# Merging attention and feed-forward sums of three query chunks, and sending score tiles in pairs by another rule, in a fused transformer block

## The chip, the cores and the metric

The kernel runs on one core of one Trainium2 chip. The metric is the device time of one execution in microseconds (us). A core has TensorE (PE, with its weight loads PEld), VectorE (DVE), ScalarE (ACT), GpSimd (POOL) and SyncE (SP, which issues the DMAs here). The records also give for each run the mean clock that was granted to TensorE, as a share of full speed.

## The reference, cut to what matters

```python
# x: 1 x 2048 x 512 (bf16); 32 heads of 16; feed-forward width 1792
xn = layernorm(x)
q, k, v = split(xn @ wqkv)
p = softmax(einsum("bhqd,bhkd->bhqk", q, k) * 16 ** -0.5)
attn = einsum("bhqk,bhkd->bhqd", p, v) @ wo
h = silu(xn @ w1) * (xn @ w3)
return x + attn + h @ w2
```

Of the kernel before, what the change touches and what calls it, by code (L numbers as in the profile page):

```python
# [9 lines left out]
ALU = mybir.AluOpType  # L10
# [1027 lines left out]
def _plan_fast(nc, ps, flag, A_x, A_wqkv, A_wo, B_w1, B_w3, B_w2, out):  # L1038
# [15 lines left out]
    NR = NU * RPU  # L1054
    NV = NU + 1
    NPR = 12
    NON = 6
    NP = NG // 2
    G_LO = 352.0
# [14 lines left out]
    A_SOON = 0.7  # L1074
    D_SOON = 0.6
    D_RIDE = 1.0
    A_OVER = 0.1
    A_EARLY = 0.1
    WARM = 36
    VB0 = 24  # L1080
# [10 lines left out]
    with ctx:  # L1091
# [8 lines left out]
        lnt = sb("lnt", [128, NT], FP32)  # L1100
        mhalf = sb("mhalf", [128, NT], FP32)
        xnT = sb("xnT", [128, DC, S], BF16)
        hT = sb("hT", [128, FC, 512], BF16)
        wq = sb("wq", [128, DC, D], BF16)
        wkv = sb("wkv", [128, 2, DC, D], BF16)
        wk = wkv[:, 0]
# [428 lines left out]
        def tiles_FFN(sc, fc):  # L1535
            idx = sc * FC + fc
            sl = idx % NW
            ss = idx % 2

            def mk(which):  # L1540
                gr = []
                for c in range(DC):
                    gr.append((lambda e, bk, c=c: col_groups(
                        lambda i: w13[:, sl, which * DC + c, 32 * i:32 * i + 32],
                        xnT[:, c, sc * 512:(sc + 1) * 512], 512)(e, bk, c == 0, c == DC - 1),
                        [("w13", sl, which)] + xk(sc * 512, 512), None, DG))
                return gr

            def start():
                if idx + NW - 1 < NQC * FC:  # L1550
                    P.post("sp", lambda: load_w13(idx + NW - 1), ready=P.t, prio=3)

            def evac_g(bk, o, rel):
                def e1():
                    q = P.op("act", lambda e: e.activation(th[:, ss, :], bank(bk), ACTF.Tanh, scale=0.5),  # L1555
                             reads=[("ps", bk)], writes=[("th", ss)], dur=a_cost(512))

                    def e2():
                        q2 = P.op("dve", lambda e: e.scalar_tensor_tensor(t1[:, ss, :], th[:, ss, :], 1.0, bank(bk),  # L1559
                                                                          ALU.add, ALU.mult),  # L1560
                                  reads=[("th", ss), ("ps", bk)], writes=[("t1", ss)], dur=d_cost(512))
                        done[("t1", idx)] = q2.end
                        rel(q2)
                    P.post("dve", e2, ready=q.end + _LAT, prio=1)
                P.post("act", e1, ready=o.end + _LAT, prio=0)

            def evac_u(bk, o, rel):
                def e1():
                    q = P.op("dve", lambda e: e.scalar_tensor_tensor(hT[:, fc, :], t1[:, ss, :], 0.5, bank(bk),  # L1569
                                                                     ALU.mult, ALU.mult),  # L1570
                             reads=[("t1", ss), ("ps", bk)], writes=[("hT", fc)], dur=d_cost(512))
                    done[("hT", sc, fc)] = q.end + _LAT
                    rel(q)
                P.post("dve", e1, ready=o.end + _LAT, prio=1, cond=lambda: ("t1", idx) in done)

            def cond_g():
                if not have(("w13", idx)):
                    return False
                if not xdone(sc * 512, 512)():
                    return False  # L1580
                if sc > 0 and not all(("HF", (sc - 1) * 4 + i) in done for i in range(4)):
                    return False
                return True
            return [_T("G%d_%d" % (sc, fc), mk(0), evac_g, cond=cond_g, start=start),
                    _T("Y%d_%d" % (sc, fc), mk(1), evac_u, cond=lambda: ("G%d_%d" % (sc, fc)) in done)]

# [9 lines left out]
        def tile_OUT(tg, part):  # L1596
            qc, ts = divmod(tg, 4)

            def og(g, slot, key):
                return (lambda i: onorm[:, slot, ts * 128 + 32 * i:ts * 128 + 32 * i + 32], wo[:, g, :],  # L1600
                        [("ON", slot, ts // 2), ("wor", g)],
                        lambda: have(key))
            ffn = [(lambda i, fc=fc: hT[:, fc, ts * 128 + 32 * i:ts * 128 + 32 * i + 32], w2[:, fc, :],
                    [("hT", fc), ("w2", fc)], None) for fc in range(FC)]
            ats = [og(g, (qc * NP + g) % NON, ("ON", qc, g)) for g in range(NP)]
            last_b = [og(NP - 1, ON_B, ("ON", qc, "B", ts // 2))]
            res = [(lambda i: ident[:, 32 * i:32 * i + 32], xr[:, ts % 2, :], [("ident",), ("xr", ts % 2)],
                    lambda: have(("xl", tg)))]
            na = NP - 2 if ts < 1 else NP - 1
            gr = {2: ats[na:] + last_b, 3: ffn + ats[:na] if qc == NQC - 1 else ffn, 4: ats,  # L1610
                  5: ffn + res + ats + last_b}[part]
            groups = []
            for k, (lh, rh, rd, cd) in enumerate(gr):
# [2 lines left out]
            def evac(bk, o, rel):  # L1616
                def e1(eng="dve"):
                    if part == 3:
# [4 lines left out]
                        done[("XE", tg)] = q.end  # L1623
                        rel(q)
                        return
                    if part == 5:
                        q = P.op("act", lambda e: e.activation(osb[:, ts, :], bank(bk), ACTF.Identity),
                                 reads=[("ps", bk)], writes=[("osb", ts), ("xn", ts)], dur=a_cost(512))
                    else:
                        q = P.op("dve", lambda e: e.tensor_tensor(osb[:, ts, :], bank(bk), osum[:, ts, :], ALU.add),  # L1630
                                 reads=[("ps", bk), ("osum", ts)], writes=[("osb", ts), ("xn", ts)], dur=d_cost(512))
                    rel(q)
                    done[("XE", tg)] = q.end
                    if part == 4:
                        P.post("sp", lambda: P.dma(lambda e: e.dma_start(out_v[:, tg, :], osb[:, ts, :]),
                                                   reads=[("osb", ts)], writes=[("out", tg)], kb=128),
                               ready=q.end + _LAT, prio=1)
                        return
# [7 lines left out]
                if part == 5:  # L1646
                    P.post("act", lambda: e1("act"), ready=o.end + _LAT, prio=1)
                else:
                    P.post("dve", e1, ready=o.end + _LAT, prio=1, cond=lambda: part in (2, 4) or ("xr", tg) in done)

            def cond():
                if part == 4:
                    return have(("OSUM", tg), ("ON", qc, NP - 1))
                if part == 2:
                    return have(("OSUM", tg)) and late()
                if not have(*[("hT", qc, fc) for fc in range(FC)]):
                    return False
                if part == 3 and qc > 0 and ("OUT", (qc - 1) * 4 + ts) not in done:
                    return False
                if part == 3:  # L1660
                    return have(*[("KTm", NP - 1, i_) for i_ in range(NQC)])
                return part == 5 or have(("ON", qc, NP - 1))

            def start():
# [2 lines left out]
                    done[("xr", tg)] = P.t  # L1667
                    done[("xl", tg)] = P.dma_last[(P.ndma - 1) % _NDMA_SEMS].end + 0.5
                P.post("sp", load, ready=P.t, prio=1, cond=lambda: tg < 2 or ("XE", tg - 2) in done)
            return _T("O%d_%d" % (tg, part), groups, evac, cond=cond, start=None if part in (2, 4) else start)  # L1670


        st = {"dbl": 0, "pos": 0, "pv": 0, "dbal": 0, "nd": 0, "lastA": -1.0, "n_exp": 0, "wait_a": 0, "hold_d": 0, "last_par": 0, "p1_at": -1.0, "p1_op": None}
# [41 lines left out]
        for sc in range(NQC):  # L1715
            for fc in range(FC):
                bg.extend(tiles_FFN(sc, fc))
            if sc > 0:
                for ts in range(4):
                    bg.append(tile_OUT(sc * 4 - 4 + ts, 4))  # L1720
            for ts in range(4):
                bg.append(tile_OUT(sc * 4 + ts, 5 if sc == NQC - 1 and ts > 2 else 3))
        for ts in range(3):
            bg.append(tile_OUT((NQC - 1) * 4 + ts, 2))
        bank_free = {b: 0.0 for b in range(7)}
# [98 lines left out]
        def try_a():  # L1824
# [7 lines left out]
                    return False  # L1832
                st["dbl"] = 2
            two = len(free) > 1
            if not two and not st["early"]:
                due = max(P.t, P.free["act"]) + 0.905 * st["wait_a"] - A_SOON
                if due > P.t and sorted(pbuf)[1] <= due + A_OVER:
                    return False
# [3 lines left out]
            if two and not st["early"]:  # L1842
                one_a(free[1], st["last_par"])
            return True

        def one_a(buf, avoid):
            nx = a_next(avoid)
# [38 lines left out]
            return None  # L1886

        def d_due():
            if P.free["dve"] - P.t > (D_RIDE if P.pem[0] == "row" and P.t < P.pem[2] + 0.1 else D_SOON):
                return False  # L1890
            sl = dcur[0]
            if sl is None:
# [314 lines left out]
        def start_tile(urgent_only):  # L2207
# [10 lines left out]
                tl = src[2]  # L2218
            elif not urgent_only:
                tl = None  # L2220
                cand = bg[:4 if st["pos"] >= NR else 3] + [x for x in bg[3:] if x.name[0] == "O" and x.name.endswith("_4")]
                if cand and any(z[0] == 0 for z in crit[:4]):
                    cand = []
                cand.sort(key=lambda x: not x.name.endswith("_4"))
                for x in cand:
                    if x.cond is None or x.cond():
                        tl = x
                        break
                if tl is None:
                    return  # L2230
                bg.remove(tl)
            else:
                return
# [7 lines left out]
        def try_dense():  # L2241
            start_tile(False)
            for a in active:
# [6 lines left out]
                if not a.groups:  # L2250
# [5 lines left out]
                    if a.name[0] == "O":  # L2256
                        tg_, pt_ = a.name[1:].split("_")
                        if pt_ != "3":
                            done[("OUT", int(tg_))] = o.end
                        if pt_ in "35":  # L2260
                            done[("HF", int(tg_))] = o.end
                    a.evac(bk, o, rel)
                return True
            return False
# [144 lines left out]
```

## The kernel before: the parts that the change touches

The program is static. A planner written in Python runs through a model of the five engines, decides at each moment what every engine issues next, and so fixes the order on every engine; the times of its model only choose that order. 2048 queries are cut into four chunks of 512. Scores are made in tiles of 128x1024 (two heads' groups side by side, two PSUM banks). Such a tile goes either to ACT, one exponential, or to DVE, which builds an approximate exponential from integer steps: a first step `p1` out of PSUM for each tile, then four steps m, t, g, e on two tiles together. There are three PSUM buffers for score tiles (six banks), one bank for dense work and one for the product with V.

How a score tile for ACT or DVE is sent (cut):

```python
def try_a():
    ...
    two = len(free) > 1                       # free: score buffers that are empty
    if not two and not st["early"]:
        due = max(P.t, P.free["act"]) + 0.905 * st["wait_a"] - A_SOON
        if due > P.t and sorted(pbuf)[1] <= due + A_OVER:      # A_SOON 0.7, A_OVER 0.1
            return False                      # another buffer comes free soon: wait, send two
    ...
def d_due():
    if P.free["dve"] - P.t > (D_RIDE if P.pem[0] == "row" and P.t < P.pem[2] + 0.1 else D_SOON):
        return False                          # D_SOON 0.6, D_RIDE 1.0
    ...
```

Two score tiles that are sent one after the other form one run of row-tiled matmuls on TensorE (row-tiled, 32*128 in the lists of groups: each matmul has 32 input rows and is placed at one of the rows 0, 32, 64, 96 of TensorE's array; column-tiled, 128*32 or 128*17 there, as nearly everything else here: 32 output rows or fewer, placed at one of the columns 0, 32, 64, 96).

The output tiles (cut). For every 128 rows of a chunk, the feed-forward product was summed in one PSUM group (part 3, 14 groups of four column matmuls) and moved with the residual to `osum` by DVE; later the attention product was summed in another (part 4, four groups) and a second DVE instruction added `osum`:

```python
hT = sb("hT", [128, FC, 512], BF16)           # FC = 14 hidden-state slots: one chunk
...
gr = {2: ats[na:] + last_b, 3: ffn + ats[:na] if qc == NQC - 1 else ffn, 4: ats,
      5: ffn + res + ats + last_b}[part]
...
if part == 3:
    q = P.op("dve", lambda e: e.tensor_tensor(osum[:, ts, :], bank(bk), xr[:, ts % 2, :], ALU.add), ...)
...
else:
    q = P.op("dve", lambda e: e.tensor_tensor(osb[:, ts, :], bank(bk), osum[:, ts, :], ALU.add), ...)
```

The hidden state of the next chunk could be written as soon as part 3 of this chunk had read the slots; attention did not have to be through.

## Time and profile before

| | kernel before |
|---|---|
| median of the first three runs (range) | 790.03 us (788.83 to 790.27) |
| busy: PE, DVE, ACT | 95%, 97%, 98% of 788.1 us |
| exponentials on ACT; score tiles on DVE | 796; 228 |
| DVE sums of 128x512 for the output | 30 |
| score runs on PE (instruction order) | 745 |

A line of the groups reads: source line, engine, operation, output<-input, shapes, count; then busy time in us and the mean of one in ns; then the engine's idle time just before them and what ended most of it. The prediction below shows the lines.

### The profile page before, as it was taken

The page shows a single profiled execution, that of the slowest core. Times are in us where ns is not written, and L with a number is a line of the kernel's source. Part 1 is how long each engine was busy: PE and PEld are TensorE (multiplying, and loading weights), DVE is VectorE, ACT ScalarE, POOL GpSimd, SP SyncE. Part 2 cuts the span into 40 slices and gives each one's busy share as a digit, 9 for nine tenths or more (in the row PEclk, how much of TensorE's full clock was granted, in tenths as well). Part 3 has the DMA queues.
Part 4 walks back from the last instruction along what each step waited for, and adds up shares of the span by engine and source line. Part 5 has one row for each costly group of instructions (what it writes and reads, how often), then busy time and mean ns, then how long its engine had stood idle before and what let it go on. Part 6 is the DMA issues. An engine that isn't in the chain of part 4 may idle for free.

```text
span 788.1 us, 21640 instructions
## 1 busy us (share of the span) xinstructions
PE 747.1 (95%) x9337; PEld 226.8 (29%) x9337; DVE 764.8 (97%) x1023; ACT 768.5 (98%) x870; POOL 90.7 (12%) x120
## 2 busy tenths in 40 slices
PE   8999999999999999999999999999899999999997
PEld 6422222222222222222222222222222222222234
DVE  8899999999999999999999999999999999999995
ACT  6999999999999999999999999999999999999994
POOL 3200021002020010201102020010201103010000
PEclk9999999999999999999999999999999999999999
DMA  7023122322332222333302234322222332232121
GB/s 215 2 22 115 9 36 30 49 21 40 51 43 22 30 41 38 47 49 45 50 14 34 22 55 56 41 35 38 34 29 23 56 43 39 49 52 16 20 25 33
DMA packets 83441, 32.94 MB, mean 42 GB/s; under 512 B 72072, under 2 KB 79496, under 8 KB 83336
## 3 DMA queue, kind: packets, MB, share of 16 engines
q1 hardware_dynamic: 83336, 31.46, 28.0%
q8 instruction: 75, 1.23, 0.6%
q14 instruction: 30, 0.25, 0.1%
HBM read 22.81 MB, written 2.10 MB: 32 GB/s over the span
## 4 chain that ended last, share of the span: by engine, by line
ACT 82%; PE 11%; DVE 5%; issue 0%; DMA 0%; POOL 0%; DVEq 0%; ACTq 0%
ACT f_PT L1866 78%; PE ps L1332 4%; PE ps L1803 4%; ACT f_th L1555 3%; PE ps L2066 3%; DVE f_xd L1939 1%; DVE f_xd L1988 1%; DVE f_xd L2003 0%; DVE f_xd L1981 0%; DMA f_xd<-in_A_x_dram 0%; DVE f_hT L1569 0%; PE ps L1344 0%; DVE f_t L1559 0%; DVE f_stats L1256 0%; DVE f_xd L1997 0%
## 5 line engine op out<-in xcount | busy, mean ns | idle before, releaser
L1866 ACT ACTIVATE f_PT<-ps 128x1024 bf16<-128x1024 f32 x796 | 744.7, 1151 | 3.4 <-PE ps L1803 3.2
L1803 PE MATMUL ps<-f_QT,f_KT 32*128 32x512 bf16 (+1 forms) x2112 | 313.6, 378 | 23.3 <-ACT f_PT L1866 17.2
L1939 DVE TENSOR_SCALAR f_xd<-ps 128x1024 int16<-128x1024 f32 x228 | 277.2, 1216 | 2.8 <-PE ps L1803 2.5
L2066 PE MATMUL ps<-f_PT,f_Vaug 128*17 128x512 bf16 (+2 forms) x1640 | 205.1, 378 | 1.1 <-DVE f_U L2086 0.5
L2066 PE MATMUL ps<-f_xd,f_Vaug 128*32 128x512 bf16 (+2 forms) x1416 | 181.9, 377 | 4.6 <-DVE f_U L2086 3.1
L1803 PEld LDWEIGHTS ps<-f_QT,f_KT 32*128 32x128 bf16 x2112 | 80.5, 91 | 322.0 <-ACT f_PT L1866 262.1
L1332 PE MATMUL ps<-f_xnT,f_w 128*32 128x512 bf16 x1792 | 143.1, 386 | 3.7 <-DVE f_t L1559 1.6
L1988 DVE TENSOR_TENSOR f_xd<-f_xd 128x2048 bf16<-128x2048 bf16 (+1 forms) x115 | 139.7, 1215 | 0.0
L1471 POOL TENSOR_SCALAR f_QT<-f_QT,f_msk 128x256 bf16<-128x256 bf16 x60 | 55.3, 922 | 270.5 <-DVE f_xd L1997 112.8
L1981 DVE TENSOR_SCALAR f_xd<-f_xd 128x2048 int16<-128x2048 int16 (+1 forms) x115 | 78.1, 679 | 3.9 <-PE ps L2066 3.1
L2003 DVE TENSOR_SCALAR f_xd<-f_xd 128x2048 int16<-128x2048 int16 (+1 forms) x115 | 78.3, 681 | 0.0
L1997 DVE TENSOR_SCALAR f_xd<-f_xd 128x2048 int16<-128x2048 int16 (+1 forms) x115 | 78.2, 680 | 0.0
L1332 PE MATMUL ps<-f_w,f_hT 128*32 128x512 bf16 x896 | 73.2, 383 | 0.2 <-DVE f_xn_sb L1630 0.2
L2127 POOL TENSOR_TENSOR f_onorm<-f_U,f_R 128x256 bf16<-128x256 f32 x30 | 25.4, 854 | 375.6 <-DMA f_R<-f_Rrow 255.0
L2066 PEld LDWEIGHTS ps<-f_PT,f_Vaug 128*32 128x32 bf16 (+1 forms) x1640 | 51.3, 92 | 58.6 <-issue 45.1
L2066 PEld LDWEIGHTS ps<-f_xd,f_Vaug 128*32 128x32 bf16 (+1 forms) x1416 | 46.1, 92 | 49.0 <-issue 28.5
L1332 PEld LDWEIGHTS ps<-f_xnT,f_w 128*32 128x32 bf16 x1792 | 36.6, 95 | 65.2 <-issue 56.5
L1555 ACT ACTIVATE f_th<-ps 128x512 f32<-128x512 f32 x56 | 40.4, 722 | 0.0
L1569 DVE SCALAR_TENSOR_TENSOR f_hT<-f_t,ps 128x512 bf16<-128x512 bf16 x56 | 37.9, 678 | 1.2 <-PE ps L1332 0.8
L1559 DVE SCALAR_TENSOR_TENSOR f_t<-f_th,ps 128x512 bf16<-128x512 f32 x56 | 37.9, 676 | 0.2
L1332 PEld LDWEIGHTS ps<-f_w,f_hT 128*32 128x32 bf16 x896 | 19.1, 95 | 23.1 <-issue 16.4
L1332 PE MATMUL ps<-f_wo,f_onorm 128*32 128x512 bf16 x272 | 22.1, 383 | 0.3 <-DVE f_wkv L1619 0.2
(82 smaller groups left out, 246.1 us busy)
## 6 DMA issues: line engine op xcount, KB each, us to landing
f_w<-in_B_w_dram SPq DMA_DIRECT2D x112, 128.0 KB
f_R<-f_Rrow SPq DMA_DIRECT2D x124, 32.0 KB
f_xr<-in_A_x_dram SPq DMA_DIRECT2D x16, 128.0 KB
f_U<-f_U SPq DMA_DIRECT2D x60, 32.0 KB
f_w<-in_B_w_dram SPq DMA_DIRECT2D x7, 256.0 KB
f_xd<-in_A_x_dram SPq DMA_DIRECT2D x3, 512.0 KB
out_dram<-f_xn_sb SPq DMA_DIRECT2D x12, 128.0 KB
f_xd<-in_A_x_dram SPq DMA_DIRECT2D x2, 256.0 KB
```

The lines of the kernel that those rows point to most:

```text
L1332: ins = e.matmul(bank(bk)[32 * i:32 * i + 32, 0:ncols], make_lhsT(i), rhs_ap, start=start, stop=stop, tile_position=(0, 32 * i))
L1471: q = P.op("pool", lambda e: e.tensor_scalar(QT[:, d_, cs], QT[:, s1, cs], msk[:, h:h + 1], None, ALU.mult), reads=[("QT", s1), ("msk", h) ...
L1555: q = P.op("act", lambda e: e.activation(th[:, ss, :], bank(bk), ACTF.Tanh, scale=0.5), reads=[("ps", bk)], writes=[("th", ss)], dur=a_cos ...
L1559: q2 = P.op("dve", lambda e: e.scalar_tensor_tensor(t1[:, ss, :], th[:, ss, :], 1.0, bank(bk), ALU.add, ALU.mult), reads=[("th", ss), ("ps ...
L1803: ins = e.matmul(b, l_, r_, start=True, stop=True, tile_position=(rp, 0))
L1866: q = P.op("act", lambda e: e.activation(PT[:, s_, :], ps[:, b0 * 512:(b0 + 2) * 512], ACTF.Exp, scale=ASC, bias=ABIAS), reads=[("ps", b0) ...
L1939: q = P.op("dve", lambda e: e.tensor_scalar(dsl[:, ys, 1024 * c:1024 * c + 1024], ps[:, b0 * 512:b0 * 512 + 1024], YB, G_LO, ALU.add, ALU. ...
L1981: P.op("dve", lambda e: e.tensor_scalar(dsl[:, NY + m_, 0:n], y, 0x7F, 0x3F00, ALU.bitwise_and, ALU.bitwise_or), reads=YK, writes=[("ds", ...
L1988: q_ = P.op("dve", lambda e: e.tensor_tensor(t_ap.bitcast(BF16), y.bitcast(BF16), t_ap.bitcast(BF16), ALU.mult), reads=YK + [("ds", NY + m ...
L1997: q_ = P.op("dve", lambda e: e.tensor_scalar(g_ap, y, -G_LO, 0.0, ALU.add, ALU.max), reads=YK, writes=[("g", g_, k) for k in range(n // 51 ...
L2003: q_ = P.op("dve", lambda e: e.tensor_scalar(y, y, 0x7F80, None, ALU.bitwise_and), reads=YK, writes=YK, dur=s_cost(n), name="e", lock=True)
L2066: ins = e.matmul(bank(PV)[32 * j:32 * j + (17 if g % 2 == 0 else 32), pc], v_, p_, start=s0, stop=s1, tile_position=(0, 32 * j))
```

## The change

It has two parts. First, for the first three chunks the feed-forward and the attention product go into one PSUM group (part 0) that DVE moves once, together with the residual. Since the group must wait for attention of its chunk, the ring of hidden-state slots grows from 14 to 20, so the feed-forward part can run six slots ahead. Second, another rule decides when a single score tile is held back for a partner: ACT's tile longer (0.4 us over its due time instead of 0.1), DVE's tile also; with two buffers free, DVE's tile may go 1.4 us ahead of its due time instead of 0.6; and a tile that can join a row run just started is not held. The aim is less DVE work, and fewer switches between row and column tiles on TensorE (in the chain before, eight column matmuls that followed scores took 0.55 us, at 0.22 us per four otherwise).

```diff
+    NH = 20
...
-    A_OVER = 0.1
+    D_TWO = 1.4
+    D_OVER = 0.3
+    A_OVER = 0.4
...
-        hT = sb("hT", [128, FC, 512], BF16)
+        hT = sb("hT", [128, NH, 512], BF16)
...
-                if sc > 0 and not all(("HF", (sc - 1) * 4 + i) in done for i in range(4)):
+                if idx >= NH and not all(("OUT", (idx - NH) // FC * 4 + i) in done for i in range(4)):
                     return False
...
-            gr = {2: ats[na:] + last_b, 3: ffn + ats[:na] if qc == NQC - 1 else ffn, 4: ats,
+            gr = {0: ffn + ats, 2: ats[na:] + last_b, 3: ffn + ats[:na] if qc == NQC - 1 else ffn,
                   5: ffn + res + ats + last_b}[part]
...
+                    if part == 0:
+                        q = P.op("dve", lambda e: e.tensor_tensor(osb[:, ts, :], bank(bk), xr[:, ts % 2, :], ALU.add),
...
-            if not two and not st["early"]:
+            if not two and not st["early"] and not riding():
                 due = max(P.t, P.free["act"]) + 0.905 * st["wait_a"] - A_SOON
...
         def d_due():
-            if P.free["dve"] - P.t > (D_RIDE if P.pem[0] == "row" and P.t < P.pem[2] + 0.1 else D_SOON):
+            n = len(open_bufs())
+            if P.free["dve"] - P.t > (D_RIDE if riding() else D_TWO if n > 1 else D_SOON):
+                return False
+            if n == 1 and not riding() and sorted(pbuf)[1] <= P.free["dve"] + D_OVER:
                 return False
...
-                cand = bg[:4 if st["pos"] >= NR else 3] + [x for x in bg[3:] if x.name[0] == "O" and x.name.endswith("_4")]
+                rest = [x for x in bg if not x.name.endswith("_0")]
+                cand = [x for x in bg if x.name.endswith("_0")] + rest[:4 if st["pos"] >= NR else 3]
```

(`riding()` says that a row run was started within the last 0.1 us.)

More of the change, by code (lines that the diff above doesn't have):

```diff
@@ L1568, in e1 @@
                 def e1():
-                    q = P.op("dve", lambda e: e.scalar_tensor_tensor(hT[:, fc, :], t1[:, ss, :], 0.5, bank(bk),
+                    q = P.op("dve", lambda e: e.scalar_tensor_tensor(hT[:, idx % NH, :], t1[:, ss, :], 0.5, bank(bk),
                                                                      ALU.mult, ALU.mult),
-                             reads=[("t1", ss), ("ps", bk)], writes=[("hT", fc)], dur=d_cost(512))
+                             reads=[("t1", ss), ("ps", bk)], writes=[("hT", idx % NH)], dur=d_cost(512))
                     done[("hT", sc, fc)] = q.end + _LAT
@@ L1602, in og @@
                         lambda: have(key))
-            ffn = [(lambda i, fc=fc: hT[:, fc, ts * 128 + 32 * i:ts * 128 + 32 * i + 32], w2[:, fc, :],
-                    [("hT", fc), ("w2", fc)], None) for fc in range(FC)]
+            ffn = [(lambda i, fc=fc: hT[:, (qc * FC + fc) % NH, ts * 128 + 32 * i:ts * 128 + 32 * i + 32], w2[:, fc, :],
+                    [("hT", (qc * FC + fc) % NH), ("w2", fc)], None) for fc in range(FC)]
             ats = [og(g, (qc * NP + g) % NON, ("ON", qc, g)) for g in range(NP)]
@@ L1625, in e1 @@
                         return
-                    if part == 5:
+                    if part == 0:
+                        q = P.op("dve", lambda e: e.tensor_tensor(osb[:, ts, :], bank(bk), xr[:, ts % 2, :], ALU.add),
+                                 reads=[("ps", bk), ("xr", ts % 2)], writes=[("osb", ts), ("xn", ts)], dur=d_cost(512))
+                    elif part == 5:
                         q = P.op("act", lambda e: e.activation(osb[:, ts, :], bank(bk), ACTF.Identity),
@@ L1633, in e1 @@
                     done[("XE", tg)] = q.end
-                    if part == 4:
+                    if part == 0:
                         P.post("sp", lambda: P.dma(lambda e: e.dma_start(out_v[:, tg, :], osb[:, ts, :]),
@@ L1648, in evac @@
                 else:
-                    P.post("dve", e1, ready=o.end + _LAT, prio=1, cond=lambda: part in (2, 4) or ("xr", tg) in done)
+                    P.post("dve", e1, ready=o.end + _LAT, prio=1, cond=lambda: part == 2 or ("xr", tg) in done)
             def cond():
-                if part == 4:
-                    return have(("OSUM", tg), ("ON", qc, NP - 1))
                 if part == 2:
@@ L1656, in cond @@
                 if not have(*[("hT", qc, fc) for fc in range(FC)]):
-                    return False
-                if part == 3 and qc > 0 and ("OUT", (qc - 1) * 4 + ts) not in done:
                     return False
@@ L1669, in start @@
                 P.post("sp", load, ready=P.t, prio=1, cond=lambda: tg < 2 or ("XE", tg - 2) in done)
-            return _T("O%d_%d" % (tg, part), groups, evac, cond=cond, start=None if part in (2, 4) else start)
+            return _T("O%d_%d" % (tg, part), groups, evac, cond=cond, start=None if part == 2 else start)
         st = {"dbl": 0, "pos": 0, "pv": 0, "dbal": 0, "nd": 0, "lastA": -1.0, "n_exp": 0, "wait_a": 0, "hold_d": 0, "last_par": 0, "p1_at": -1.0, "p1_op": None}
@@ L1717, in _plan_fast @@
                 bg.extend(tiles_FFN(sc, fc))
-            if sc > 0:
-                for ts in range(4):
-                    bg.append(tile_OUT(sc * 4 - 4 + ts, 4))
             for ts in range(4):
-                bg.append(tile_OUT(sc * 4 + ts, 5 if sc == NQC - 1 and ts > 2 else 3))
+                bg.append(tile_OUT(sc * 4 + ts, 0 if sc < NQC - 1 else 5 if ts > 2 else 3))
         for ts in range(3):
@@ L1844, in try_a, with riding @@
             return True
+        def riding():
+            return P.pem[0] == "row" and P.t < P.pem[2] + 0.1
         def one_a(buf, avoid):
@@ L2220, in start_tile @@
                 tl = None
-                cand = bg[:4 if st["pos"] >= NR else 3] + [x for x in bg[3:] if x.name[0] == "O" and x.name.endswith("_4")]
+                rest = [x for x in bg if not x.name.endswith("_0")]
+                cand = [x for x in bg if x.name.endswith("_0")] + rest[:4 if st["pos"] >= NR else 3]
                 if cand and any(z[0] == 0 for z in crit[:4]):
                     cand = []
-                cand.sort(key=lambda x: not x.name.endswith("_4"))
                 for x in cand:
@@ L2259, in try_dense @@
                             done[("OUT", int(tg_))] = o.end
-                        if pt_ in "35":
-                            done[("HF", int(tg_))] = o.end
                     a.evac(bk, o, rel)
```

## The prediction

> **What bounds the kernel now.** I read the busy times first. Three engines are nearly full at once, so the page alone does not name the bound.
>
> ```profile
> span 788.1 us, 21640 instructions
> ...
> PE 747.1 (95%) x9337; PEld 226.8 (29%) x9337; DVE 764.8 (97%) x1023; ACT 768.5 (98%) x870; POOL 90.7 (12%) x120
> ```
>
> ScalarE (ACT) lacks 788.1 - 768.5 = 19.6 us. Cut into 40 us windows, ACT is busy 40.00 of 40.00 us in all but four of twenty. Of the idle time, 8.1 us lie in the first 30 us, 1.3 us between 280 and 320 us, and the rest at the end. The groups and the waits of ACT say the same:
>
> ```profile
> L1866 ACT ACTIVATE f_PT<-ps 128x1024 bf16<-128x1024 f32 x796 | 744.7, 1151 | 3.4 <-PE ps L1803 3.2
> L1939 DVE TENSOR_SCALAR f_xd<-ps 128x1024 int16<-128x1024 f32 x228 | 277.2, 1216 | 2.8 <-PE ps L1803 2.5
> L1803 PE MATMUL ps<-f_QT,f_KT 32*128 32x512 bf16 (+1 forms) x2112 | 313.6, 378 | 23.3 <-ACT f_PT L1866 17.2
> ```
>
> ```profile
> ACT f_PT L1866 <- PE ps L1803: 3.2, 5, 1.3
> ```
>
> A score tile (128x1024) goes to ACT for an exponential (796 of 1024) or to VectorE (DVE) for an integer approximation (228). Ahead of all 796 exponentials ACT waited for scores only five times, 3.2 us in all. The score matmuls, by contrast, wait for ACT to empty a PSUM buffer. So ACT paces the steady part. The third view is the chain of work that ended last:
>
> ```profile
> 30.43 82.58 ACT f_PT L1866 x90
> 113.50 6.42 ACT f_PT L1866 x7
> 120.41 9.17 ACT f_PT L1866 x10
> ...
> 739.06 0.22 PE ps L1332 x4
> 739.28 0.33 PE ps L1803 x4
> 739.61 0.76 PE ps L2066 x12
> 740.36 0.32 PE ps L1803 x2
> 740.68 0.55 PE ps L1332 x8
> ```
>
> 82.58 / 90 gives the true price of an exponential: 0.917 us, not the mean of 1151 ns, since neighbours overlap. Between two runs 120.41 - (113.50 + 6.42) = 0.49 us pass: that is one tanh of the feed-forward part. The chain stays on ACT to about 730 us, then on TensorE (PE) to 780 us; both are full there. Last, a stretch of the timeline of DVE gives its prices, from start to start:
>
> ```profile
> 755.05 0.68 DVE L1619 TENSOR_TENSOR f_wkv<-ps,f_xr 128x512 f32<-128x512 f32 x1
> 755.64 1.21 DVE L1939 TENSOR_SCALAR f_xd<-ps 128x1024 int16<-128x1024 f32 x1
> 756.78 0.68 DVE L2086 COPY f_U<-ps 128x512 f32<-128x512 f32 x1
> 757.37 0.68 DVE L1981 TENSOR_SCALAR f_xd<-f_xd 128x2048 int16<-128x2048 int16 x1
> 757.97 0.68 DVE L1997 TENSOR_SCALAR f_xd<-f_xd 128x2048 int16<-128x2048 int16 x1
> 758.58 1.21 DVE L1939 TENSOR_SCALAR f_xd<-ps 128x1024 int16<-128x1024 f32 x1
> ```
>
> A 128x512 sum out of PSUM costs 0.60 us, the first step on a score tile 1.14, and a step on two tiles (128x2048) 0.60; the product in the chain (L1988) costs 1.13 by the same reading. Two tiles on DVE so cost 2 x 1.14 + 1.13 + 3 x 0.60 = 5.21 us; a chain of one tile 1.14 + 0.60 + 3 x 0.34 = 2.76 us.
>
> [...] Scores use row tiles, everything else here column tiles. [...] a score run of one tile (x2) or of two (x4) costs 0.32 to 0.33 us alike. Column matmuls cost about 0.22 us per four, and a column run that follows scores some 0.11 us more (x8 0.55, x12 0.76). [...] in the waits its score loads stand still for ACT's release 628 times.
>
> **The change part by part.** I counted the instructions of both built programs, engine by engine.
>
> *Merged groups.* For the first three query chunks (12 row tiles) the feed-forward and attention products now accumulate in one PSUM group, with one DVE sum instead of two; hidden-state slots grow from 14 to 20 so that the feed-forward part may run ahead while attention finishes. Of the 128x512 sums (L1619, L1630) 30 become 18: DVE sheds 12 x 0.60 = 7.2 us. No matmul goes. One 128x384 copy of V moves from DVE (0.46 us, estimated from 0.60 for 512 and 0.34 for 256 columns) to ACT (0.45 us, between the starts of L1385 and L1403). DVE is relieved by 7.66 us.
>
> *What the scheduler does with it.* Scores on DVE go from 228 to 231 and exponentials from 796 to 793; chains of two tiles from 113 to 115, of one tile from 2 to 1. DVE gains 2 x 5.21 - 2.76 = 7.66 us: its work is unchanged. ACT changes by -3 x 0.917 + 0.45 = **-2.3 us**. ACT being the pacemaker, this is the gain to expect; the tile is cheap on ACT and dear on DVE, so 7.7 us of DVE time buy only 2.3 us.
>
> *Pairing.* A single score tile for ACT or DVE is held back if a second buffer comes free soon, so that two are sent as one row run. Score runs on PE fall from 745 to 703 (runs of x2 from 464 to 394, x4 from 258 to 275). At 0.32 us, plus 0.11 for the column run that no longer restarts, 42 runs are 18 us of PE time. In the steady part that lies beside ACT's work and is worth nothing by itself. It can take away the 1.3 us that ACT idled near 310 us and the 0.36 us ahead of its last three exponentials: together 1.7 us, of which I count **-0.7 us**. In the last eighth of the scores, runs fall from 75 to 67 and other matmuls from 748 to 716: 8 x 0.43 + 8 x 0.22 = 5.2 us less PE work there, enough that PE should not hold ACT's 2.3 us back.
>
> *The end.* From the last exponential (777.46 us) to 788.1 us there are 10.6 us of sums, normalisation, last products and the store; the order there is nearly the same, and I leave it. Against the gain I set **+0.2 us** for waits that the holding rule brings.
>
> Sum: 790.0 - 2.3 - 0.7 + 0.2 = **787.2 us**.
>
> **The rivals.** (a) PE is the true bound, since the chain lies on it for 50 us and it shows 95%: then 18 us come off and the time is near 772 us, faster by over 2%. For it speaks the chain after 730 us; against it, that ACT hardly waits for scores and is full until 774 us, so only ACT's own work can shorten it. (b) Holding starves ACT or DVE. ACT's tile is held to at most 0.3 us before it is due (0.7 early, 0.4 over), while the trace has 0.36 us from issue to use (PE at 774.07, ACT at 774.43): under 0.1 us for a hold, and only when held to the limit. With, say, 40 such holds ACT loses 2 to 3 us and the gain is gone: 790 us. On DVE the bubble can be larger, but other steps of the chain lie ready to fill it. (c) The merged group waits for the last normalised attention of its chunk, and the feed-forward part can only run six slots ahead: dense work could pile up at the end and make PE the bound, 792 to 795 us. Against it: after the last tanh the changed order has 62 exponentials, before 55, so the feed-forward part ends no later.
>
> **Range and chances.** Runs of the kernel before spread over 1.4 us. ACT's counts are fixed by the program, so the gain has a ceiling of some 5 us (2.3 plus all idle time between the start and the last exponential, 1.7, plus about a microsecond at the end): lower end 784.5. Rival (b) or (c) in part gives the upper end, 791.0. Two per cent is 15.8 us: faster by that would need rival (a) against the zero idle of ACT (0.01); slower would need stalls that the order does not suggest (0.02).
>
> **What would show it.** In the profile after: 793 exponentials at about 0.917 us in long runs, ACT's busy time lower by about 2 us; 18 sums of 128x512; waits of ACT for scores no more than some 3 us; PE's busy time or its score groups lower by more than 10 us with little effect on the span; the last exponential near 774.5 us with some 10.6 us behind it. If ACT's waits for scores grow to 5 us or more, (b) was right; if the chain lies on PE from earlier than 730 us, (c); a span below 780 us would make ACT's pacing wrong.

## The result and the profile after

The changed kernel took 788.04 us (median of six, 787.58 to 790.04), the kernel before in the same rounds 790.04 us (788.83 to 790.57). The ratio is 0.9984, 95% interval 0.9969 to 0.9999: the same within 2%, and inside the predicted range. (Ratios here are the mean time of one kernel's fast runs over that of the other's of the same rounds, so not quite the ratio of the quoted medians.)

The page of the changed kernel, busy times and the three groups shown before, and from its list of groups the merged sums (12; the last chunk keeps 3 and 3, so 18 in all):

```profile
span 786.1 us, 21663 instructions
...
PE 734.9 (93%) x9353; PEld 227.6 (29%) x9353; DVE 764.1 (97%) x1017; ACT 766.9 (98%) x868; POOL 91.9 (12%) x120
...
L1868 ACT ACTIVATE f_PT<-ps 128x1024 bf16<-128x1024 f32 x793 | 742.3, 1124 | 2.0 <-PE ps L1802 1.7
L1802 PE MATMUL ps<-f_QT,f_KT 32*128 32x512 bf16 (+1 forms) x2112 | 296.4, 378 | 30.9 <-ACT f_PT L1868 26.0
L1944 DVE TENSOR_SCALAR f_xd<-ps 128x1024 int16<-128x1024 f32 x231 | 280.7, 1215 | 4.2 <-PE ps L1802 3.3
L1630 DVE TENSOR_TENSOR f_xn_sb<-ps,f_xr 128x512 bf16<-128x512 f32 x12 | 8.2, 684 | 0.5 <-PE ps L1335 0.5
```

TensorE lost 12 us of busy time and the score matmuls 17 us (313.6 to 296.4), yet the span fell by 2.0 us only; ACT's busy time fell by 1.6 us, with three exponentials fewer. So far this is as predicted. ACT's waits for scores, in the list of waits:

```profile
ACT f_PT L1868 <- PE ps L1802: 1.7, 4, 0.6
```

They fell from 3.2 to 1.7 us. But the reason is not the one predicted. The prediction took a wait of 1.3 us near 310 us for something that pairing could remove. A finer cut of the kernel before (columns: stretch, its length, busy time and count of PE, PEld, DVE, ACT and POOL, then granted clock, DMA share, GB/s) shows what it was:

```profile
304.00:306.00 2.00, 2.00 (x24) 0.50 (x16) 2.00 (x4) 2.00 (x4) 0.00 (x0) 1.00 0.08 17
306.00:308.00 2.00, 1.30 (x10) 0.38 (x8) 2.00 (x3) 2.00 (x4) 0.00 (x0) 1.00 0.00 0
308.00:310.00 2.00, 1.61 (x16) 0.53 (x18) 1.90 (x3) 2.00 (x4) 0.00 (x0) 0.62 0.04 4
310.00:312.00 2.00, 2.00 (x24) 0.49 (x16) 1.11 (x3) 1.09 (x2) 0.00 (x0) 0.52 0.25 53
```

From 308.5 us on TensorE had half its clock for 3.4 us (0.50 from 308.50 to 311.92 us; 0.62 and 0.52 are means over the stretches), and ACT and DVE starved. Such a stretch is called a dip below. Just before, at 306 to 308 us, TensorE had only ten matmuls in 2 us. The profiled execution of the changed kernel happened to have no such dip. A first look at the six runs of the changed kernel agreed: 787.58 to 788.11 us at a mean clock of 0.997 to 0.999, 789.91 and 790.04 us at 0.992 and 0.993. So the comparison of two profiles, and even of two medians, mixes the change with dips.

The end of ACT's timeline, before and after:

```profile
774.43 3.03 ACT L1866 ACTIVATE f_PT<-ps 128x1024 bf16<-128x1024 f32 x3 [0.36 <-PE ps L1803]
778.69 0.38 ACT L2160 ACTIVATE f_U<-ps 128x256 f32<-128x256 f32 x1 [1.23 <-PE ps L2066]
```

```profile
717.34 57.42 ACT L1868 ACTIVATE f_PT<-ps 128x1024 bf16<-128x1024 f32 x62
776.75 0.38 ACT L2165 ACTIVATE f_U<-ps 128x256 f32<-128x256 f32 x1 [1.99 <-PE ps L2071]
```

The last exponential ends at 777.46 us before and at 774.76 us after, 2.7 us earlier. Behind it 10.6 us remained before and 11.3 us remain now: more products with V are queued on TensorE at that moment (40 of their matmuls start between the last exponential and L2165, before it was 20; the wait ahead of L2165 is 1.99 us, it was 1.23). The last long piece on ACT in the chain of work that ended last reaches to 751.5 us, where it was 730:

```profile
717.57 33.93 ACT f_PT L1868 x37
```

### The profile page after: what moved, and what is told of

Its sections match the earlier page's. It is cut to its first block, busy times and chain, and to the rows that moved or that the text cites. A ratio compares the mean times of both kernels' runs of the same rounds, so it can differ in the third digit from the quotient of the medians.

```text
span 786.1 us, 21663 instructions
## 1 busy us (share of the span) xinstructions
PE 734.9 (93%) x9353; PEld 227.6 (29%) x9353; DVE 764.1 (97%) x1017; ACT 766.9 (98%) x868; POOL 91.9 (12%) x120
## 4 chain that ended last, share of the span: by engine, by line
ACT 79%; PE 13%; DVE 6%; issue 1%; DMA 0%; POOL 0%; DVEq 0%; ACTq 0%
ACT f_PT L1868 76%; PE ps L1335 5%; PE ps L1802 4%; ACT f_th L1558 3%; PE ps L2071 3%; DVE f_xd L1944 2%; DVE f_xd L1993 1%; DVE f_xd L2002 1%; DMA f_xd<-in_A_x_dram 0%; DVE f_xd L1986 0%; DVE f_xd L2008 0%; DVE f_hT L1572 0%; PE ps L1347 0%; DVE f_stats L1259 0%; PE ps L1494 0%
## 5 line engine op out<-in xcount | busy, mean ns | idle before, releaser
L1802 PE MATMUL ps<-f_QT,f_KT 32*128 32x512 bf16 (+1 forms) x2112 | 296.4, 378 | 30.9 <-ACT f_PT L1868 26.0
L1944 DVE TENSOR_SCALAR f_xd<-ps 128x1024 int16<-128x1024 f32 x231 | 280.7, 1215 | 4.2 <-PE ps L1802 3.3
L1802 PEld LDWEIGHTS ps<-f_QT,f_KT 32*128 32x128 bf16 x2112 | 75.6, 91 | 315.0 <-ACT f_PT L1868 258.1
L1335 PE MATMUL ps<-f_xnT,f_w 128*32 128x512 bf16 x1792 | 138.1, 383 | 3.7 <-DVE f_hT L1572 1.9
L1993 DVE TENSOR_TENSOR f_xd<-f_xd 128x2048 bf16<-128x2048 bf16 x116 | 141.1, 1216 | 0.0
L1986 DVE TENSOR_SCALAR f_xd<-f_xd 128x2048 int16<-128x2048 int16 x116 | 79.2, 683 | 2.5 <-PE ps L2071 1.9
L2008 DVE TENSOR_SCALAR f_xd<-f_xd 128x2048 int16<-128x2048 int16 x116 | 80.0, 689 | 0.0
L2002 DVE TENSOR_SCALAR f_xd<-f_xd 128x2048 int16<-128x2048 int16 x116 | 79.5, 686 | 0.0
L1335 PEld LDWEIGHTS ps<-f_xnT,f_w 128*32 128x32 bf16 x1792 | 38.5, 94 | 63.4 <-issue 49.4
L1335 PEld LDWEIGHTS ps<-f_w,f_hT 128*32 128x32 bf16 x896 | 17.5, 94 | 23.5 <-issue 18.4
```

The costliest lines, as they stand in the source:

```text
L1335: ins = e.matmul(bank(bk)[32 * i:32 * i + 32, 0:ncols], make_lhsT(i), rhs_ap, start=start, stop=stop, tile_position=(0, 32 * i))
L1802: ins = e.matmul(b, l_, r_, start=True, stop=True, tile_position=(rp, 0))
L1944: q = P.op("dve", lambda e: e.tensor_scalar(dsl[:, ys, 1024 * c:1024 * c + 1024], ps[:, b0 * 512:b0 * 512 + 1024], YB, G_LO, ALU.add, ALU. ...
L1986: P.op("dve", lambda e: e.tensor_scalar(dsl[:, NY + m_, 0:n], y, 0x7F, 0x3F00, ALU.bitwise_and, ALU.bitwise_or), reads=YK, writes=[("ds", ...
L1993: q_ = P.op("dve", lambda e: e.tensor_tensor(t_ap.bitcast(BF16), y.bitcast(BF16), t_ap.bitcast(BF16), ALU.mult), reads=YK + [("ds", NY + m ...
L2002: q_ = P.op("dve", lambda e: e.tensor_scalar(g_ap, y, -G_LO, 0.0, ALU.add, ALU.max), reads=YK, writes=[("g", g_, k) for k in range(n // 51 ...
```

## The experiments

The theory after the result: ACT's instruction count sets the undisturbed time, the room on TensorE is worth little, and dips of TensorE's clock, which the pairing makes more frequent, eat what is gained. The rivals: the pairing's TensorE time is the gain; VectorE is the pacemaker; the dips are chance. The chip was the same within each session, not across sessions. Every one of the twelve runs gave a correct result.

| run | what | median us | ratio to before (95%) | runs with mean clock under 0.998 | median us of the others |
|---|---|---|---|---|---|
| before, two sessions | | 789.20 | 1 | 5 of 22 | 789.09 |
| changed, three sessions | first result, e4, e9 | 789.10 | 0.9984, 1.001, 0.9988 | 12 of 18 | 787.68 |
| e1_merge_only | merged groups, old rule | 790.16 | 1.001 (0.9997 to 1.0023) | 2 of 5 | 789.17 |
| e2_pair_only | new rule, old groups | 790.31 | 1.0006 (0.9993 to 1.0018) | 5 of 6 | 788.21 (one run) |
| e3_slots14 | changed, 14 slots | 807.26 | 1.0224 (1.0205 to 1.0243) | 5 of 5 | none |
| e5_fill_same | changed + 67 fillers | 789.14 | 0.9995 (0.9981 to 1.0009) | 1 of 5 | 789.18 |
| e10_fill33 | changed + 33 fillers | 788.18 | 0.9984 (0.9971 to 0.9996) | 1 of 6 | 788.30 |
| e12_fill13 | changed + 13 fillers | 788.47 | 0.9985 (0.9972 to 0.9997) | 4 of 6 | 787.90 |
| e6_act_plus | changed + 12 us on ACT | 802.20 | 1.0164 (1.0148 to 1.0179) | 4 of 4 | none |
| e7_dve_plus | changed + 13 us on DVE | 800.23 | 1.0126 (1.0105 to 1.0147) | 3 of 4 | 797.81 (one run) |
| e8_pe_plus | changed + 12 us on PE | 792.94 | 1.0042 (1.0026 to 1.0057) | 3 of 4 | 792.40 (one run) |
| e11_pe_plus_before | before + 12 us on PE | 792.80 | 1.0038 (1.0023 to 1.0054) | 0 of 4 | 792.80 |

The clocks of the kernel before in the first session were not recorded, so its 22 runs come from the two later sessions. The line at 0.998 was drawn after seeing the runs; it sorts by clock, not by time. The profiled executions bear it out: the kernel before, with one dip of 3.4 us, has 0.997, the changed kernel, with none, 0.999. Runs at 0.998 or more are called undisturbed.

**e1_merge_only, one half of the change.** Against the changed kernel:

```diff
-    A_OVER = 0.4
+    A_OVER = 0.1
-            if not two and not st["early"] and not riding():
+            if not two and not st["early"]:
-            if P.free["dve"] - P.t > (D_RIDE if riding() else D_TWO if n > 1 else D_SOON):
-                return False
-            if n == 1 and not riding() and sorted(pbuf)[1] <= P.free["dve"] + D_OVER:
+            if P.free["dve"] - P.t > (D_RIDE if riding() else D_SOON):
                 return False
```

> Merged groups and 20 hidden-state slots, but the old rule of due times. The program has 795 exponentials and 229 score tiles on VectorE, so VectorE got 7.2 us lighter and ScalarE only 0.9 us. Theory (ScalarE paces, its count of exponentials decides): 0.5 to 1.5 us faster than the kernel before, ratio about 0.999. Rival 1 (VectorE is the pacemaker and the 7.2 us come off it): 782 to 784 us. Rival 2 (the pairing is what brought the gain): no difference from before.

Measured: 790.16 us, 789.17 us in the runs at 0.998 or more, against 789.09 us for the kernel before. VectorE is not the pacemaker by itself: 7.2 us of sums came off it (3.3 us of its busy time, 764.8 to 761.5, since it has one score tile more) and nothing came of it. The expected gain of 0.9 us for one exponential was not seen either; with three such runs, spread over 1.1 us, a difference of this size stays open. In its profile the stretch from the first exponential to the last is 1.5 us shorter than in the kernel before (763.1 against 764.6 us, the latter with the dip), but it starts 0.5 us later (12.4 against 11.9 us; 11.9 to 12.5 over all fourteen profiles), and the end is 0.3 us longer.

**e2_pair_only, the other half.** The hunks of the diff above that touch `A_OVER`, `D_TWO`, `D_OVER`, `riding` and `d_due`, put into the kernel before.

> The new rule of due times alone, groups as before (14 slots, two sums for each row tile). 794 exponentials, 705 score runs on TensorE instead of 745, so 40 x 0.43 = 17 us less TensorE time. Theory: TensorE time beside ScalarE's work is worth nothing, so -2 x 0.917 + 0.45 = -1.4 us at best, and less if the holding costs: between 0 and -1.4 us. Rival (TensorE is the bound): about 773 us.

Measured: 790.31 us. 17 us less TensorE time by count (its score matmuls are busy for 300.3 us instead of 313.6) did not bring 773 us, so TensorE is not the bound. Five of six runs are under 0.998, of the kernel before on the same chip 3 of 11: the dips come with the pairing. Windows of its profiled execution:

```profile
732.00:736.00 4.00, 3.23 (x26) 0.86 (x26) 4.00 (x6) 4.00 (x5) 0.00 (x0) 1.00 0.05 9
736.00:740.00 4.00, 3.89 (x28) 0.73 (x26) 4.00 (x6) 3.72 (x5) 0.00 (x0) 0.52 0.15 30
740.00:753.00 13.00, 12.96 (x88) 2.50 (x86) 10.24 (x13) 10.62 (x11) 1.45 (x2) 0.50 0.31 21
```

A stretch with few matmuls (26 in 4 us) is followed by 17 us at half clock (0.50 to 0.52 up to 753 us), in which ACT stands for 2.4 of 13 us. The one run at 0.998 took 788.21 us, 0.9 us under the kernel before: within the expected 0 to 1.4 us, from a single run; the median of all six is 1.2 us over it.

**e3_slots14, the ring of slots.**

```diff
-    NH = 20
+    NH = 14
```

> The changed kernel with 14 hidden-state slots instead of 20: the feed-forward part of the next chunk can't begin before attention of its chunk is finished and the merged sums are through. Exponentials and sums are the same as in the changed kernel (793, 18). Theory (c of the prediction's rivals is real but the ring of 20 slots avoids it): dense work piles up and stalls or lengthens the end, 4 to 12 us slower than the changed kernel. If the ring is not needed: the same time as the changed kernel within 1 us.

Measured: 807.26 us, some 18 us slower than the changed kernel: the direction was right, the size under-estimated. Exponentials and score tiles are the same in number (793 and 231). Its profile (mean clock 0.983) has 27 us of half clock in four dips, of which the longest begins at 396 us:

```profile
396.00:400.00 4.00, 4.00 (x22) 0.69 (x18) 3.17 (x4) 3.25 (x4) 0.00 (x0) 0.50 0.00 0
400.00:410.00 10.00, 9.92 (x62) 1.80 (x62) 6.92 (x9) 7.39 (x8) 0.00 (x0) 0.54 0.07 14
```

and dense work piled up at the end, where ACT's last instruction waits 12.2 us for it instead of 3.4:

```profile
798.35 0.60 ACT L1633 ACTIVATE f_xn_sb<-ps 128x512 bf16<-128x512 f32 x1 [12.20 <-PE ps L1335]
```

So the merged groups are only possible with the larger ring: without it dense work is missing in the middle, where TensorE then runs at half clock (0.50 to 0.54 from 396 to 410 us), and is left over at the end.

**e4_after_again and e9_after_third, the changed kernel itself.**

> The changed kernel unaltered, beside the others on the same chip, to compare them with: 786.5 to 788.5 us in runs without a dip of the granted clock, ratio about 0.998. If dips of the granted clock make the 2 us difference between its runs, the runs near 790 us must be those with a mean clock under 0.995.

> The changed kernel unaltered again, as partner of the next run on the same chip. If the pairing lets the clock dip, about half of its runs or more show a mean clock under 0.998 and take 789 us or more, and those at 0.998 or more take 787.5 to 788.3 us. If the dips of the earlier chip were chance, nearly all runs are at 0.998 or more and near 788 us.

Measured: 789.48 us and 1.001 (0.9994 to 1.0027) in e4, 788.88 us and 0.9988 (0.9972 to 1.0004) in e9. Over the three sessions the eighteen runs sort by clock: 787.32 to 788.12 us at 0.998 or more (6 runs), 788.07 to 789.28 us at 0.996 and 0.997 (4), 789.69 to 790.04 us at 0.992 to 0.994 (6), 791.65 and 792.28 us at 0.989. The expectation held in kind: runs of 789.69 us and more are those under 0.995. 12 of 18 are under 0.998, of the kernel before 5 of 22. Undisturbed the change brings 789.09 - 787.68 = 1.4 us; in the median of all runs 0.1 us.

**e5_fill_same, taking the suspected cause away.** Zero weights are multiplied into the open sum of the product with V, which adds 0.0, so that TensorE has something to do; the order of everything else is that of the changed kernel.

```diff
+        zw = sb("zw", [128, 32], BF16)          # zeros
...
+        def fill():
+            ...                                 # a sum is open, TensorE idle, no score tile possible for 0.4 us
+            def f(e):
+                for j in range(4):
+                    ins = e.matmul(bank(PV)[32 * j:32 * j + (17 if g % 2 == 0 else 32), :], zw[:, 0:17 if g % 2 == 0 else 32],
+                                   xnT[:, 0, 0:512], start=False, stop=False, tile_position=(0, 32 * j))
+                return ins
```

> The changed kernel in its own order on every engine, with 67 extra groups of four TensorE matmuls with zero weights (they add 0.0 to an open sum) in places where TensorE would stand idle for at least 0.4 us. 67 x 0.22 = 15 us more TensorE work, nothing else. Theory (pairing left TensorE so idle in places that its clock is granted at half for spans of 3.4 us, and these dips eat the gain): mean clock 0.998 or more in most runs, 787.5 to 788.5 us in the median, ratio about 0.998 to 0.999, while the changed kernel itself had 0.989 to 0.998 and 789.5 us on this chip. Rival (dips come by chance or from the chip, not from TensorE's idle time): the same clocks as the changed kernel and 789 to 791 us.

Measured: clocks 0.997 to 0.999 in all five runs, where the changed kernel on the same chip (e9) has 0.992 to 0.999. At most a short dip is left in one run, so the dips come from TensorE's thin stretches and not from chance alone. The time, 789.14 us, was a miss: 0.3 us better than the changed kernel in e4, on another chip, 0.3 us worse than in e9, and not the 787.5 to 788.5 us expected. Part of this is outside the program: device time less span is 2.5 us in the mean of these runs, in all other kernels 1.7 to 1.8, for which I have no reason. By span, 786.45 us (median of its undisturbed runs) stand against 785.95 for undisturbed runs of the changed kernel: the fillers cost about 0.5 us.

**e10_fill33 and e12_fill13, fewer fillers.** They are kept to places where few groups of TensorE were issued in the 3 us before:

```diff
+            if sum(o_.end > P.t - 3.4 + 0.4 for o_ in P.ops["pe"][-40:]) >= 12:      # 11 in e12_fill13
+                return False
```

> The changed kernel in its own order with 33 zero-weight groups of four matmuls instead of 67: only where TensorE would stand idle for at least 0.4 us and few of its groups (under 12) were issued in the 3 us before. Theory ([...]the 67 fillers cost about 1 us by being in the way elsewhere): clocks of 0.998 or more in most runs, and 787.8 to 788.6 us in the median, ahead of both the kernel before (789.1) and the changed kernel. Rival (fillers don't matter): clocks and times as in the unaltered changed kernel beside it.

> As the kernel with 33 zero-weight groups, but only where fewer than 11 of TensorE's groups (not 12) were issued in the 3 us before: 13 groups. Undisturbed runs of the changed kernel took 787.4 us on that chip, and 788.3 with 33 groups. Theory (each group costs a little, and only the emptiest windows bring a dip): clocks still 0.998 or more in most runs, median 787.6 to 788.2 us, ratio about 0.998. If 13 groups are too few: clocks under 0.998 in half of the runs and 788.5 us or more.

Measured: with 33 fillers 788.18 us with a spread of 0.6 us (787.91 to 788.52) and 0.997 to 0.999 in all six runs, while the changed kernel beside it spread from 787.32 to 789.95 us. This is the version with the best median of its session: 788.18 us against 788.88 for the changed kernel and 789.15 for the kernel before. Its lead over the kernel before is clear of noise (interval 0.9971 to 0.9996), that over the changed kernel is not settled. With 33 or 67 fillers 2 of 11 runs are under 0.998, of the changed kernel beside them 4 of 6. With 13 fillers 4 of 6 are again, but none under 0.995: too few, the second case of the expectation. Its two undisturbed runs take 787.90 us. Fillers cost a little in an undisturbed run: 0.1 us of span (786.1) with 13, 0.65 us (786.6) with 33 and 0.5 us with 67, over 785.95. The same stretch of the trace in e4 and in e10 fits the cause. First e4:

```profile
602.00:604.00 2.00, 1.48 (x14) 0.42 (x14) 2.00 (x3) 2.00 (x3) 0.92 (x1) 1.00 0.91 37
604.00:606.00 2.00, 1.30 (x12) 0.30 (x12) 2.00 (x3) 2.00 (x4) 0.07 (x1) 1.00 0.22 68
606.00:608.00 2.00, 1.73 (x18) 0.49 (x18) 2.00 (x4) 2.00 (x4) 2.00 (x2) 0.85 0.01 4
608.00:610.00 2.00, 2.00 (x18) 0.45 (x18) 1.80 (x3) 1.79 (x2) 0.75 (x3) 0.50 0.00 0
```

Then e10:

```profile
602.00:604.00 2.00, 1.79 (x20) 0.52 (x18) 2.00 (x3) 2.00 (x3) 0.92 (x1) 1.00 0.91 29
604.00:606.00 2.00, 1.69 (x18) 0.40 (x16) 2.00 (x3) 2.00 (x3) 0.44 (x1) 1.00 0.34 79
606.00:610.00 4.00, 3.63 (x48) 1.01 (x44) 4.00 (x5) 4.00 (x6) 1.02 (x2) 1.00 0.00 2
```

26 matmuls in 4 us, then half clock; with 38 the clock stays whole. But one pair of traces is no proof. The first profile of the changed kernel had 26 there too, and no dip:

```profile
602.00:604.00 2.00, 1.48 (x14) 0.42 (x14) 2.00 (x3) 2.00 (x4) 0.92 (x1) 1.00 0.85 35
604.00:606.00 2.00, 1.30 (x12) 0.30 (x12) 2.00 (x3) 2.00 (x4) 0.19 (x1) 1.00 0.22 68
606.00:608.00 2.00, 1.79 (x20) 0.58 (x20) 2.00 (x4) 2.00 (x3) 2.00 (x2) 1.00 0.02 4
```

TensorE was not idle in them: before the dip of e4 it was busy for 2.78 of the 4 us, in the first profile of the changed kernel for as long. So the program makes the thin stretches, and whether one of them brings a dip differs from execution to execution. What shows the cause are the counts of runs with and without fillers.

**e6_act_plus, e7_dve_plus, e8_pe_plus and e11_pe_plus_before: the same load on each engine.** Each adds about 12 us to one engine, in 56 pieces beside the feed-forward work, and leaves the order alone.

```diff
+  e.activation(spare[:, ss, 0:192], bank(bk)[:, 0:192], ACTF.Tanh, scale=0.5)                  # e6, ahead of each tanh
+  e.scalar_tensor_tensor(spare[:, ss, 0:160], th[:, ss, 0:160], 1.0, bank(bk)[:, 0:160],
+                         ALU.add, ALU.mult)                                                    # e7, ahead of t1
+  if c == 0 and which == 0:
+      g(e, bk, True, True)                              # e8 and e11: first group of each gate tile twice
```

> The changed kernel with 56 extra activations of 192 columns on ScalarE, one ahead of each tanh, order unchanged: about 56 x 0.22 = 12 us more ScalarE work (0.45 us for 384 columns and 0.49 for 512 in the traces). Theory (ScalarE paces): nearly all of it appears, 9 to 13 us slower than the changed kernel, about 799 us. If ScalarE has hidden slack: under 6 us.

> The changed kernel with 56 extra VectorE instructions of 160 columns beside the feed-forward ones, order unchanged: about 56 x 0.24 = 13 us more VectorE work (0.60 us for 512 columns, 0.34 for 256). Theory (VectorE is as full as ScalarE, so a fixed order can't absorb it): 8 to 13 us slower, about 798 us. If VectorE has slack beside ScalarE: under 4 us.

> The changed kernel with 56 extra groups of four column matmuls, the first group of each gate tile computed twice: 56 x 0.22 = 12 us more TensorE work, in the feed-forward stretches. Theory (TensorE has slack beside ScalarE): 0 to 4 us slower, or even even with it if dips of the clock go away. Rival (TensorE is the bound): 12 us slower, 800 us.

> The kernel before with the 56 extra groups of four column matmuls that cost the changed kernel 3.5 to 5 us: 12 us more TensorE work. Theory (pairing gave TensorE room that the merged kernel can use, so the kernel before has less of it): 5 to 10 us slower than the kernel before, ratio 1.006 to 1.013. Rival (TensorE has the same room in both): the same 3.5 to 5 us.

The pieces cost what the timelines of e6 and of e7 show from start to start, 0.21 us and 0.23 us, so 11.8 and 12.9 us in all:

```profile
114.98 0.45 ACT L1560 ACTIVATE f_spare<-ps 128x192 bf16<-128x192 f32 x1
115.19 0.72 ACT L1561 ACTIVATE f_th<-ps 128x512 f32<-128x512 f32 x1
```

```profile
115.89 0.32 DVE L1564 SCALAR_TENSOR_TENSOR f_spare<-f_th,ps 128x160 bf16<-128x160 f32 x1
116.12 0.69 DVE L1566 SCALAR_TENSOR_TENSOR f_t<-f_th,ps 128x512 bf16<-128x512 f32 x1
```

Against 788.88 us of the changed kernel on that chip, ACT's load shows in full (+13.3 us for 11.8, all four runs with dips), DVE's nearly (+11.4 us for 12.9; +10.4 us from undisturbed to undisturbed, 797.81 - 787.44), PE's by a third (+4.1 us for 12; +5.0 us undisturbed, 792.40 - 787.44). ACT's load was expected to cost 9 to 13 us, TensorE's 0 to 4: both came out slightly above. ACT sets the time, DVE is almost as tight in a fixed order, TensorE has room. The last run refutes what I expected of it: the kernel before loses the same 3.7 us (792.80 - 789.15), so an added load finds no more room after the pairing than before it. All four runs of the kernel before with added TensorE work are at 0.998 or more; but of the changed kernel with the same work (e8) only one of four is, and its profile (mean clock 0.995) has a dip at 610.5 us. Work beside the feed-forward part does not fill the thin stretches, as the fillers do.

## Why the prediction was right or wrong, point by point

The predicted 787.2 us was right within its range (784.5 to 791.0): 788.04 us at first, 789.48 and 788.88 us in the later sessions. Undisturbed runs, 787.68 us in the median, are closest to it. That the first comparison came so near to the predicted gain (2.0 us of 2.8) was in part luck: the kernel before stood at 790.04 us in that session, at 789.20 us in the two later ones, where the changed kernel is level with it. Its steps:

- **ACT paces: right.** e6 shows added ACT work in full. The sign for rival (c), the chain on TensorE from before 730 us, came only for 609 to 644 us, and at the end the chain stays on ACT longer than before; from 534 to 562 and from 644 to 662 us it lies mostly on DVE. ACT loses no more there than elsewhere: its steps above 904 ns sum to at most 0.4 us in each 20 us, and 0.35 us is the mean of the whole steady part. The long runs of exponentials have the 0.917 us per tile that was read; but start to start, the median of neighbouring exponentials in the trace is 904 ns, and 0.917 already contains small gaps that the idle column does not show, since the recorded durations overlap (neighbouring exponentials by 201 ns in the median after, 247 ns before). A busy share of 98% so hides most of the 13.28 us of such gaps that are counted below.
- **Counts, -2.3 us: right.** 793, 231 and 18 are there. Three exponentials at 0.904 us are -2.71 us, the other ACT instructions in between +0.36 us, together -2.35 us.
- **Pairing is beside ACT's work and worth nothing by itself: right, but one size and one consequence were missed.** The estimated -0.7 us for ACT's waits rested on a wait that was a dip of the clock in that one execution. From the start of an exponential to the next start on ACT, the time above 904 ns sums to 13.90 us before and 13.28 us after; the 0.6 us between them is about what the dip cost that execution (788.1 us against 787.4 in the median of undisturbed runs). That the term came out near its estimate was luck: one profile had a dip, the other none. Undisturbed, it is about zero.
- **+0.2 us for holding (rival b): mis-sized.** Gaps of 26 to 300 ns above the median step sum to 7.8 us before and 9.3 us after, so rival (b) is real, some 1.5 us in this pair of traces; with the smaller gaps counted too it is 1.0 us (10.5 to 11.5). Other profiles agree: 8.0 us with merging alone (e1), 9.3 us with pairing alone (e2), 9.3 to 9.8 us in e4, e5, e9, e10 and e12. They are not the same as the prediction's sign for it, "waits grow to 5 us": ACT's listed waits fell, because gaps under about 0.2 us, the median overlap of neighbours (201 ns), hide in overlapping durations.
- **The end unchanged: wrong by +0.65 us.** 11.29 us instead of 10.64, for the products with V that still queue on TensorE. It is no accident of one execution: 11.3 to 11.6 us in e4, e9, e10 and e12, 10.7 us in e11, the kernel before with added work.
- **The sum.** In the two profiles: start of the steady part +0.27, counts -2.35, gaps -0.62, end +0.65, together -2.05 us, as the spans say. Undisturbed, the gain is 1.4 us.
- **Rival (a), TensorE as the bound: rejected** by e2 and e8, as the prediction thought. **Rival (c), dense work piling up: real, and avoided by the ring of 20 slots** (e3).
- **What no step foresaw:** room on TensorE is not only worthless, it has a price. The clock was cut to half after a thinly filled stretch (e2: 26 matmuls in 4 us, then 17 us at 0.50 to 0.52), pairing brings such stretches, and 12 of 18 runs were under 0.998, the slowest 4.6 us behind. Against that, the change's gain of 1.4 us hardly shows in the medians.

Open stay: where the exponential that merging alone saves went (e1), whether 33 fillers are ahead of the plain changed kernel over many sessions, and which exact measure of activity trips the clock; stretches as thin as those before a dip also passed without one (26 matmuls in the 4 us from 602 us in the first profile of the changed kernel, at a clock of 1.00).

## What to carry to other kernels

Where ACT paces, count ACT's instructions first; time freed on another engine is worth only what the schedule can move off ACT with it, here 2.3 us for the 7.7 us of DVE, and nothing for the 17 us of TensorE. Look at the granted clock of every run before comparing two kernels that differ by less than half a per cent, and cut the trace finely around a wait before calling it a scheduling loss. If freeing TensorE makes its stretches thin, try matmuls with zero weights in the thinnest places to hold its clock: here 33 groups sufficed (1 of 6 runs under 0.998), 13 did not (4 of 6).
